# The middle stage of a long convolution, run beside a dense matmul stream: 37 wide items where there were 64 narrow ones, and its last stage moved behind them

## The chip, the cores and the metric

The kernel runs on one core of a Trainium2 chip. TensorE (PE in the profile, PEld for its weight loads), VectorE (DVE), ScalarE (ACT), GpSimd (POOL) and SyncE (SP) run side by side. Each takes its own instructions in a fixed order, and a semaphore holds an instruction until its data is there. SP, ACT and POOL also issue the DMAs. The metric is the device time of one execution in microseconds, as the median of the runs, where lower is better.

## The reference, cut to what matters

The input is 2048 tokens of 576 channels. Two kinds of layer alternate, each twice:

```
def A(x):                                # Fourier mixing of the normalized x
    a, b = x @ dft_hid_re.T, x @ dft_hid_im.T
    return dft_seq_re @ a - dft_seq_im @ b
def B(q, k, v, shift_k, ssm_k, ssm_D):   # q is the normalized x
    kv = shift(k, shift_k) * v           # causal convolution over 4 tokens
    y = irfft(rfft(pad(kv)) * rfft(pad(ssm_k)))[:S] + kv * ssm_D   # long convolution, per channel
    return q * y
x = x + A(norm(x)); x = x + B(norm(x), ...); x = x + A(norm(x)); x = x + B(norm(x), ...)
```

The long convolution `y` depends on k, v and weights alone. It is computed once and used in both B layers.

## The kernel before, in words

**The main stream.** The first A layer (`layer`, called with `get_x0`) takes 128 steps. One step multiplies one block of x by one 128x512 block of the sequence matrix `c_mat`: 14 matmuls of 512 columns (12 into the accumulators `s0` to `s3`, 2 into `rm`). Every product is made of rounded parts: a number is split into a high part (ACT, a copy that rounds) and a low part (DVE, the rest), and three matmuls high x high, high x low, low x high stand for one. The block of `c_mat` for a step is loaded by SP two steps ahead into the ring `craw` and split into the ring `cs` (ACT line 94, DVE line 95). After every 16 steps the accumulators are emptied into `u` by the same kind of split; the remainder `rm` goes through the buffer `rt` at `RT_AT` (lines 270, 271, then a split). `hidden` multiplies a finished block by the hidden matrix: pieces of 27 matmuls of 288 columns, each followed by one DVE add (line 292).

**The branch.** `branch` is a generator that puts the convolution between these steps. Its transform of 4096 points is done as 128 x 16 in three stages.
- First transform: row blocks of k*v and of the filter are multiplied by `f1c` and stored to `t` in DRAM, until the main stream's step 45.
- Middle: an item takes four frequencies q, with 16 j and 2 complex parts on the partitions: `(q j c)` = 128 rows. `mid_kernel` transforms the filter over j (3 matmuls; then ACT copies three half tiles of 64 partitions into `kk`), `mid_signal` transforms the signal (3 matmuls; then four DVE operations form the complex product), `mid_round` splits the product, `mid_inverse` transforms back (3 matmuls, one ACT copy into `vo`) and stores to `vd`. The loaded item itself is split two items ahead (`split_feed`, ACT and DVE).
- Inverse (`i2_products`): one row j of `vd` is split and multiplied by `i2c[j]` (6 matmuls of 288 columns per half of the channels), copied and stored to `yb`.

Before, an item holds one half of the channels, `HD` = 288 columns: 2 halves x 32 groups of four q = 64 items. The inverse takes half rows, 32 of them. Ten half rows of the first half stand between the items of the second half; the other 22 come behind the items. An item's inverse is issued two items after its product (`MID_LAG`).

**What sets the order.** The branch yields a cost; the loop over `layer` resumes it at most `GROUPS` = 2 times at each half step, whenever the branch's costs spent so far are behind the planned share (`spent < work * passed / total`). So the branch is spread evenly from step 47 to step 111. A scheduling layer then fixes the order on each engine. All branch matmuls and the pieces of `hidden` write to one ring of three PSUM banks (tag `b`, names `bk`): a bank is free again when ACT or DVE has read it.

The stage uses two slots for `craw`, laid by these lines; the second is the same memory as `rt`:

```
lay(flts, lay(flts, 8, ("craw", NT, 1)), ("vo", HD, 2))
lay(flts, RT_AT, ("craw", NT, 1))
```

From step 48 on, even steps use the slot at 8 and odd steps the slot at `RT_AT`.

Of the kernel before, what the change touches and what calls it, by code (L numbers as in the profile page):

```python
# [15 lines left out]
P = 128  # L16
# [24 lines left out]
PREP = 113  # L41
MID_LAG = 2
LANDS = 3
BORDER = {J - 1: 0.5, 0: 0.75}
I2_FIRST = 38
I2_LATE = 6
I2_COST = 2.0
GROUPS = 2
# [19 lines left out]
def fnet_h3_kernel(ctx: ExitStack, tc: tile.TileContext, x, c_mat, w_re, w_im, k_pad, v, shift_k,  # L68
# [10 lines left out]
    def bank():  # L79
        return psp.tile([P, NT], F32, tag="b", bufs=3, name="bk")  # L80
# [121 lines left out]

    t_d = [dr.tile([P, J, 2, 2, HD], F32, name=f"t{h}") for h in range(2)]
    v_d = [dr.tile([P, J, 2, HD], F32, name=f"vd{h}") for h in range(2)]
    yb_d = [dr.tile([P, D], F32, name=f"yb{j}") for j in range(J)]
# [149 lines left out]
    def branch():  # L355
# [133 lines left out]
        m1 = region_b(FR, "mid")  # L489
        kk_at = 1976 + 2 * HD + LANDS * D  # L490
        at = lay(m1, 0, ("df", 2 * D, 3), ("mc", 4 * P, 1))
        fresh("land", "fc")
        fresh("craw")
        spare = at
        at = lay(m1, at, ("yf", D, 2))
        lay(m1, at, ("fc", 4 * P, 2))
# [3 lines left out]
        assert at == kk_at  # L500
        assert lay(flts, at, ("kk", D, 2)) <= RT_AT
        mc = quads(ring["mc"]())
        load_fr(mc, midc)
        lo, hi = slice(0, 64), slice(64, 128)

        def mid_half(df, o):
            ps = bank()
            mm(ps[:, :HD], mc[:, 0, :], df[0][:, o:o + HD], True, False)
            mm(ps[:, :HD], mc[:, 0, :], df[1][:, o:o + HD], False, False)
            mm(ps[:, :HD], mc[:, 1, :], df[0][:, o:o + HD], False, True)  # L510
            return ps

        last_act = []

        def act(*args, **kw):
            if last_act:
                with tc.issue_after(last_act[-1]):
                    last_act.append(nc.scalar.activation(*args, **kw).ins)  # L518
            else:
                last_act.append(nc.scalar.activation(*args, **kw).ins)  # L520
# [4 lines left out]

        def mid_kernel(df):
            pk, kk = mid_half(df, HD), two(ring["kk"]())
            act(kk[lo, 0, :], pk[lo, :HD], AF.Copy)
            act(kk[hi, 0, :], pk[lo, :HD], AF.Copy)
            act(kk[hi, 1, :], pk[hi, :HD], AF.Copy)  # L530
            return kk

        def mid_signal(df, kk):
            px = mid_half(df, 0)
            p1, p2 = kk[:, 0, :], kk[:, 1, :]
            nc.vector.tensor_tensor(p1, px[:, :HD], p1, OP.mult)
            nc.vector.scalar_tensor_tensor(p2[lo], px[hi, :HD], -1.0, p2[hi], op0=OP.mult, op1=OP.mult)  # L537
            nc.vector.tensor_tensor(p2[hi], px[lo, :HD], p2[hi], OP.mult)  # L538
            nc.vector.tensor_tensor(p1, p1, p2, OP.add)  # L539
            return p1  # L540

        def mid_round(p1):
            yf = two(ring["yf"]())
            act_split(yf[:, 0, :], yf[:, 1, :], p1)
            return yf

        def mid_inverse(hf, qg, yf):
            pv = bank()
            mm(pv[:, :HD], mc[:, 2, :], yf[:, 0, :], True, False)
            mm(pv[:, :HD], mc[:, 2, :], yf[:, 1, :], False, False)  # L550
            mm(pv[:, :HD], mc[:, 3, :], yf[:, 0, :], False, True)
            vo = ring["vo"]()
            act(vo, pv[:, :HD], AF.Copy)
            nc.scalar.dma_start(v_d[hf][4 * qg:4 * qg + 4].rearrange("q j c d -> (q j c) d"), vo)

        def i2_products(hf, j, fc, vf):
            yo = ring["vo"]()
            ps = bank()
            for c in range(2):
                cs = slice(c * HD, (c + 1) * HD)  # L560
# [6 lines left out]
        mids = [(0, hf, qg) for hf in range(2) for qg in range(32)]  # L567
        late = [(1, 0, j) for j in range(J)]
        feeds = []
        for g, f in enumerate(mids):  # L570
            feeds.append(f)
            if g >= I2_FIRST and (g - I2_FIRST) % 2 == 0 and len(late) > I2_LATE:
                feeds.append(late.pop(0))
        feeds += late + [(1, 1, j) for j in range(J)]
        last_mid = feeds.index(mids[-1])
        rows = [f[2] for f in feeds if f[0]]
        landed, halves, fcs, yfs = {}, {}, {}, []

        def load_feed(i):
            if i < len(feeds):  # L580
                kind, hf, q = feeds[i]
                landed[i] = ring["land"]()
                load_after(landed[i], v_d[hf][:, q].rearrange("p c d -> p (c d)") if kind else
                           t_d[hf][4 * q:4 * q + 4].rearrange("q j c s d -> (q j c) (s d)"))

        def load_fc(k):
            if k < len(rows):
                fcs[k] = quads(ring["fc"]())
                load_fr(fcs[k], i2c[rows[k]])

        def split_feed(i):
            if i < len(feeds):
                halves[i] = parts("df")
                act_split(*halves[i], landed.pop(i))

        for i in range(LANDS):
            load_feed(i)
        yield 0
        for i in range(2):
            split_feed(i)  # L600
            load_feed(i + LANDS)
            load_fc(i)
        used, ahead, product = 0, 2, None
        for i, (kind, hf, q) in enumerate(feeds):
            df = halves.pop(i)
            if kind:
                i2_products(hf, q, fcs.pop(used), df)
                load_fc(used + ahead)
                used += 1
            else:  # L610
                if len(yfs) == MID_LAG:
                    mid_inverse(*yfs.pop(0))
                    yield 0.4
                kk = mid_kernel(df)
                if product is not None:
                    yfs.append((*product[:2], mid_round(product[2])))
                yield 1.6
                product = hf, q, mid_signal(df, kk)
            split_feed(i + 2)
            load_feed(i + ahead + LANDS)  # L620
            if i == last_mid:
                yield 0.4
                mid_inverse(*yfs.pop(0))
                yfs.append((*product[:2], mid_round(product[2])))
                while yfs:
                    yield 0.4
                    mid_inverse(*yfs.pop(0))
                for name, t, at, words in (("fc", m1, spare, 4 * P), ("land", flts, kk_at, D)):
                    old = ring[name]
                    held = [old.tiles[(old.n + m) % len(old.tiles)] for m in range(len(old.tiles))]  # L630
                    fresh(name)
                    lay(t, at, (name, words, 2))
                    ring[name].tiles.extend(held)
                for m in range(2):
                    load_fc(used + ahead + m)
                    load_feed(i + ahead + LANDS + 1 + m)
                ahead = 4
            yield I2_COST if kind else 1.1

# [122 lines left out]
    total = (I2_END + 1 - MID_FROM) * STEP + 3 * 2 * TB * PIECE  # L762
    work = 64 * 3.1 + 32 * I2_COST
    for n, whole in layer(get_x0, lambda j: x[:, j, :], done0, pending):
# [30 lines left out]
        if m == 0:  # L795
            lay(flts, SC_AT + CRAW * NT + 2 * D, ("xa", D, 2), ("yb", D, 2))
            fresh("craw")
            lay(flts, SC_AT + CRAW * NT + 6 * D, ("craw", NT, 1))
# [333 lines left out]
```

## Time and profile before

| | |
|---|---|
| time, median of 3 runs | 1195.03 us (1193.86 to 1195.24) |
| time of the profiled execution | 1196.82 us, of which the span is 1195.0 us |
| PE busy | 1176.4 us, 6320 matmuls |
| DVE busy | 839.1 us |
| ACT busy | 637.3 us |
| middle and inverse stage | 203 to 612 us of the span; the last item's product is formed at 544 us |

The page gives one execution. A line of its group table reads: code line, engine, operation, output <- inputs, shape, count, then busy time and mean duration of one in ns, then the idle time of the engine just before these instructions and what ended it. Matmuls overlap, so the mean duration of one is longer than the step from one to the next.

### The profile page before, as it was taken

The page shows a single profiled execution, that of the slowest core. Times are in us where ns is not written, and L with a number is a line of the kernel's source. Part 1 is how long each engine was busy: PE and PEld are TensorE (multiplying, and loading weights), DVE is VectorE, ACT ScalarE, POOL GpSimd, SP SyncE. Part 2 cuts the span into 40 slices and gives each one's busy share as a digit, 9 for nine tenths or more (in the row PEclk, how much of TensorE's full clock was granted, in tenths as well). Part 3 has the DMA queues.
Part 4 walks back from the last instruction along what each step waited for, and adds up shares of the span by engine and source line. Part 5 has one row for each costly group of instructions (what it writes and reads, how often), then busy time and mean ns, then how long its engine had stood idle before and what let it go on. Part 6 is the DMA issues. An engine that isn't in the chain of part 4 may idle for free.

```text
span 1195.0 us, 18305 instructions
## 1 busy us (share of the span) xinstructions
PE 1176.4 (98%) x6320; PEld 1026.8 (86%) x6320; DVE 839.1 (70%) x1495; ACT 637.3 (53%) x1266; POOL 74.2 (6%) x116
## 2 busy tenths in 40 slices
PE   7999999999999999999999999999999999999997
PEld 6888888987888988888988898788888888889997
DVE  8899794588877678775447665774775776874764
ACT  7965665478766567665435656544444435540210
POOL 2200000000000000001101111000000000001111
PEclk9999999999999999999999999999999999999999
DMA  9889898546666657658947686872592587696621
GB/s 362 277 274 309 259 302 251 180 137 192 196 212 195 196 177 222 185 161 268 300 161 246 224 233 228 275 265 72 160 330 83 159 320 268 202 343 192 214 97 41
DMA packets 150719, 261.97 MB, mean 219 GB/s; under 512 B 16353, under 2 KB 53473, under 8 KB 150626
## 3 DMA queue, kind: packets, MB, share of 16 engines
q1 hardware_dynamic: 107282, 205.58, 53.9%
q10 hardware_dynamic: 36432, 42.63, 10.3%
q0 software_dynamic: 6912, 12.59, 3.9%
q8 instruction: 50, 0.82, 0.3%
q14 instruction: 43, 0.35, 0.1%
HBM read 194.09 MB, written 66.65 MB: 218 GB/s over the span
## 4 chain that ended last, share of the span: by engine, by line
PE 69%; DVE 5%; ACT 3%; DMA 2%; issue 2%; POOL 0%; ACTq 0%; SPq 0%; DVEq 0%; POOLq 0%
PE s L77 38%; PE bk L77 29%; PE rm L77 3%; DVE mid L524 1%; ACT flts L518 1%; DMA flts<-in_c_mat 1%; DVE mats L95 1%; DVE flts L538 1%; ACT mats L94 1%; DMA mid<-in_i2c 0%; DVE flts L537 0%; ACT mid L518 0%; DVE u L95 0%; DMA ph<-in_c_mat 0%; DMA gate<-xa 0%
## 5 line engine op out<-in xcount | busy, mean ns | idle before, releaser
L77 PE MATMUL s<-mats 128*128 128x512 f32 x2088 | 528.6, 392 | 2.0 <-ACT ph L867 1.5
L77 PEld LDWEIGHTS s<-mats 128*128 128x128 f32 x2088 | 380.7, 188 | 72.8 <-ACT ph L867 2.4
L95 DVE TENSOR_TENSOR mats<-flts,mats 128x512 fp32r<-128x512 f32 x201 | 137.3, 688 | 57.5 <-ACT mats L94 50.7
L94 ACT ACTIVATE mats<-flts 128x512 fp32r<-128x512 f32 x201 | 125.8, 627 | 95.2 <-PE bk L77 31.0
L518 ACT ACTIVATE flts<-bk 64x288 f32<-64x288 f32 (+1 forms) x288 | 116.0, 407 | 109.9 <-PE bk L77 93.1
L524 DVE TENSOR_TENSOR mid<-flts,mid 128x576 fp32r<-128x576 f32 (+1 forms) x160 | 102.0, 638 | 47.5 <-ACT mid L518 41.4
L77 PE MATMUL bk<-mid 128*128 128x288 f32 x768 | 128.6, 298 | 2.3 <-ACT flts L518 1.0
L77 PEld LDWEIGHTS bk<-mid 128*128 128x128 f32 x768 | 114.9, 188 | 18.0 <-ACT flts L518 5.8
L77 PE MATMUL bk<-w,u 128*128 128x288 f32 x864 | 120.2, 295 | 0.5 <-DVE flts L292 0.5
L77 PEld LDWEIGHTS bk<-w,u 128*128 128x128 f32 x864 | 117.4, 188 | 3.5 <-DVE flts L292 1.2
L77 PE MATMUL rm<-mats 128*128 128x512 f32 x304 | 94.7, 390 | 0.0
L518 ACT ACTIVATE mid<-flts 128x576 fp32r<-128x576 f32 (+1 forms) x159 | 87.0, 583 | 6.3 <-DVE flts L539 2.2
L454 ACT ACTIVATE flts<-bk 128x288 f32<-128x288 f32 x128 | 50.7, 410 | 47.1 <-PE bk L77 45.2
L77 PE MATMUL bk<-f1r 128*128 128x288 f32 x384 | 64.4, 300 | 6.5 <-ACT f1r L94 6.3
L77 PEld LDWEIGHTS bk<-f1r 128*128 128x128 f32 x384 | 59.4, 191 | 13.0 <-ACT f1r L94 6.6
L77 PE MATMUL bk<-mats 128*128 128x288 f32 (+1 forms) x376 | 67.8, 317 | 0.0
L77 PEld LDWEIGHTS rm<-mats 128*128 128x128 f32 x304 | 56.9, 188 | 12.1 <-ACT flts L518 0.2
L292 DVE TENSOR_TENSOR flts<-flts,bk 128x288 f32<-128x288 f32 x48 | 21.8, 453 | 63.6 <-PE bk L77 63.3
L77 PE MATMUL s<-t,mats 128*128 128x512 f32 x264 | 65.2, 389 | 0.0
L186 POOL TENSOR_TENSOR flts<-flts 128x1 f32<-128x1 f32 x35 | 29.6, 846 | 525.5 <-DVE flts L185 525.5
L77 PE MATMUL bk<-mats,t 128*128 128x288 f32 (+1 forms) x368 | 59.3, 303 | 0.0
L77 PEld LDWEIGHTS s<-t,mats 128*128 128x128 f32 x264 | 49.5, 188 | 10.7 <-DVE mats L200 0.4
(148 smaller groups left out, 1439.3 us busy)
## 6 DMA issues: line engine op xcount, KB each, us to landing
flts<-in_c_mat SPq DMA_DIRECT2D x148, 256.0 KB, 3.9
ph<-in_c_mat SPq DMA_DIRECT2D x54, 512.0 KB, 4.2
t<-flts ACTq DMA_DIRECT2D x64, 288.0 KB, 4.5
flts<-t SPq DMA_DIRECT2D x64, 288.0 KB, 3.2
flts<-in_c_mat SPq DMA_DIRECT2D x30, 512.0 KB, 4.8
vd<-flts ACTq DMA_DIRECT2D x64, 144.0 KB, 3.0
flts<-vd SPq DMA_DIRECT2D x32, 288.0 KB, 3.5
mid<-in_i2c POOLq DMA_DIRECT2D x32, 256.0 KB, 4.9
```

The costliest lines, as they stand in the source:

```text
L77: nc.tensor.matmul(ps, lhsT, rhs, start=first, stop=last, skip_group_check=more)
L94: a = nc.scalar.activation(h, src, AF.Copy).ins
L95: return a, nc.vector.tensor_tensor(l, src, h.bitcast(F32), OP.subtract).ins
L186: pows.append(nc.gpsimd.tensor_tensor(rs, ve, mhalf, OP.pow).ins)
L292: added[:] = [nc.vector.tensor_tensor(rows[hf], rows[hf], ps[:, :HD], OP.add).ins]
L454: stored[:] = [nc.scalar.activation(so[:, c, :], ps[:, :HD], AF.Copy).ins]
L518: last_act.append(nc.scalar.activation(*args, **kw).ins)
L524: nc.vector.tensor_tensor(l, src, h.bitcast(F32), OP.subtract)
L538: nc.vector.tensor_tensor(p2[hi], px[lo, :HD], p2[hi], OP.mult)
```

## The change

The middle stage takes 504 columns at a time: 32 items (one per group of four q) of the first 504 channels, and then 5 items that gather the last 72 channels of 7 groups each (the fifth: of 4 groups, 288 columns). The DRAM tensors `t` and `vd` hold whole rows, so that a store of the gathered items has pieces of 72 values (288 bytes) where one of 504 columns has pieces of 2016 bytes. Wide items are loaded in one buffer (`land`) or, every other one, in two pieces of 504 (`apart`), which are split one by one. An item's inverse is issued one item after its product, where it was two. `vo` has one slot, and `df` two. The inverse takes whole rows of 1152 values in two products of 288 columns, all behind the last item, with two pauses (`MID_PAUSE`) between the last item, the loads and the first row.

Core of the diff:

```diff
-MID_LAG = 2
-LANDS = 3
+MW = 504
+MID_COST = (2.1, 1.7, 1.1)
+MID_PAUSE = 4.0
-I2_COST = 2.0
+I2_COST = 2.3
...
-                nc.scalar.dma_start(t_d[hf][:, j, :, src, :], so)
+                nc.scalar.dma_start(t_d[:, j, :, src, cs], so)
...
-        at = lay(m1, 0, ("df", 2 * D, 3), ("mc", 4 * P, 1))
+        at = lay(m1, 0, ("df", 4 * MW, 2), ("mc", 4 * P, 1), ("yf", 2 * MW, 1))
+        apart = [m1[:, at:at + MW].bitcast(F32), flts[:, 8 + NT:8 + NT + MW]]
-        lay(flts, lay(flts, 8, ("craw", NT, 1)), ("vo", HD, 2))
         lay(flts, RT_AT, ("craw", NT, 1))
-        at = lay(flts, SC_AT + CRAW * NT, ("res", HD, 3), ("vo", HD, 2), ("land", D, LANDS))
+        at = lay(flts, 8, ("craw", NT, 1)) + MW
+        assert lay(flts, at, ("land", 2 * MW, 1), ("kk", MW, 4), ("vo", MW, 1)) <= RT_AT - 3 * HD
...
+        mids = [(q, 1) for q in range(groups)] + [(q, min(per, groups - q)) for q in range(0, groups, per)]
...
+        for n in range(len(mids)):
+            df, w = halves.pop(n), width(n)
+            kk = mid_kernel(df, w)
+            if n:
+                yf = mid_round(product)
+            yield MID_COST[0]
+            product = mid_signal(df, w, *kk)
+            split_mid(n + 2)
+            load_mid(n + 4)
+            yield MID_COST[1]
+            if n:
+                mid_inverse(n - 1, yf)
+                yield MID_COST[2]
+        yf = mid_round(product)
+        yield MID_COST[0]
+        mid_inverse(n, yf)
...
+        yield MID_PAUSE
+        for j in range(3):
+            load_row(j)
+        yield MID_PAUSE
+        for j in range(2):
+            split_row(j)
+            load_row(j + 3)
+        for j in range(J):
+            vf, fc = halves.pop(j), fcs.pop(j)
+            i2_products(0, j, fc, vf)
+            yield I2_COST
+            i2_products(1, j, fc, vf)
+            load_fc(j + 3)
+            split_row(j + 2)
+            load_row(j + 5)
+            yield I2_COST
...
-    work = 64 * 3.1 + 32 * I2_COST
+    work = 37 * sum(MID_COST) + 2 * MID_PAUSE + 32 * I2_COST
```

The two `craw` slots are now laid in the other order: from step 48 on, even steps use the slot that is also `rt`.

The order of TensorE changes within the stage only. The first place is the way from an item's filter transform to the inverse of the item before it. On TensorE before, `bk_3555` and `bk_3564` are filter and signal of item 29, `bk_3583` the inverse of item 27, `bk_3589` and `bk_3608` filter and signal of item 30, and `bk_3619` is the inverse of item 28:

```order
L77 MATMUL bk_3555<-mid_2080 128x288 x3
L77 MATMUL bk_3564<-mid_2080 128x288 x3
L77 MATMUL s2_68<-mats_70 128x512 x3
L77 MATMUL s3_69<-mats_70 128x512 x3
L77 MATMUL rm_3296<-mats_70 128x512 x2
L77 MATMUL bk_3583<-mid_2080 128x288 x3
L77 MATMUL bk_3589<-mid_2080 128x288 x3
L77 MATMUL s0_66<-mats_70 128x512 x3
L77 MATMUL s1_67<-mats_70 128x512 x3
L77 MATMUL bk_3608<-mid_2080 128x288 x3
L77 MATMUL bk_3619<-mid_2080 128x288 x3
```

On TensorE now, `bk_3207` and `bk_3216` are filter and signal of item 17, `bk_3238` is the inverse of item 16, and `bk_3244` the filter of item 18:

```order
L76 MATMUL bk_3207<-mid_2078 128x504 x3
L76 MATMUL bk_3216<-mid_2078 128x504 x3
L76 MATMUL s2_68<-mats_70 128x512 x3
L76 MATMUL s3_69<-mats_70 128x512 x3
L76 MATMUL rm_3102<-mats_70 128x512 x2
L76 MATMUL bk_3238<-mid_2078 128x504
L76 MATMUL bk_3244<-mid_2078 128x504 x3
L76 MATMUL bk_3238<-mid_2078 128x504 x2
```

Between the filter of item n+1 and the inverse of item n there stood 26 matmuls in the first piece, and stand 11 in the second.

The second place is SP's queue where the inverse's rows are loaded. On SP before, a load of a half row (`vd0`) stands among loads of items (`t1`), far behind the stores it needs:

```order
L168 DMA flts_72<-in_c_mat 128x512
L168 DMA flts_72<-t1_78 128x576 x2
L168 DMA flts_72<-in_c_mat 128x512
L697 DMA xa6_103<-flts_72 128x288
L284 DMA flts_72<-in_x 128x288
L168 DMA flts_72<-vd0_79 128x576
L168 DMA flts_72<-in_c_mat 128x512
```

On SP now, the first three whole rows follow the last item's loads, with loads of `c_mat` before and behind them:

```order
L167 DMA flts_72<-in_c_mat 128x512
L167 DMA flts_72<-t_77 128x4x72 x2
L167 DMA flts_72<-in_c_mat 128x512 x9
L167 DMA flts_72<-vd_78 128x1152 x3
L167 DMA flts_72<-in_c_mat 128x512 x2
L167 DMA flts_72<-vd_78 128x1152 x3
```

The first row's load waits for the store of the last gathered item. On TensorE three whole steps, 42 matmuls of 512 columns, stand between that item's inverse and the first row's product.

More of the change, by code (lines that the diff above doesn't have):

```diff
@@ new lines, in branch, with width, load_mid @@
+        per = MW // RW
+        groups = P // 4
+        mids = [(q, 1) for q in range(groups)] + [(q, min(per, groups - q)) for q in range(0, groups, per)]
+        def width(n):
+            first, count = mids[n]
+            return MW if n < groups else count * RW
+        def load_mid(n):
+            if n < len(mids):
+                first, count = mids[n]
+                w = width(n)
+                landed[n] = [r[:, :w] for r in apart] if n % 2 else [ring["land"]()[:, :2 * w]]
+                ends = landed[n] if n % 2 else [two(landed[n][0])[:, i] for i in range(2)]
+                src = t_d[4 * first:4 * (first + count)]
+                if n < groups:
+                    src = src.rearrange("q j c s d -> (q j c) s d")[:, :, :MW]
+                    if n % 2:
+                        for i in range(2):
+                            load_after(ends[i], src[:, i])
+                    else:
+                        load_after(two(landed[n][0]), src)
+                else:
+                    src = src.rearrange("(g q) j c s d -> (q j c) s g d", q=4)
+                    for i in range(2):
+                        load_after(ends[i].rearrange("p (g d) -> p g d", g=count), src[:, i, :, MW:])
@@ new lines, in split_mid, with mid_half @@
+        def split_mid(n):
+            if n < len(mids):
+                df, at = ring["df"](), 0
+                halves[n] = df[:, :2 * width(n)], df[:, 2 * MW:2 * MW + 2 * width(n)]
+                for src in landed.pop(n):
+                    cs = slice(at, at + src.shape[1])
+                    act_split(halves[n][0][:, cs], halves[n][1][:, cs], src)
+                    at = cs.stop
+        def mid_half(df, o, w):
+            ps = bank()
+            mm(ps[:, :w], mc[:, 0, :], df[0][:, o:o + w], True, False)
+            mm(ps[:, :w], mc[:, 0, :], df[1][:, o:o + w], False, False)
+            mm(ps[:, :w], mc[:, 1, :], df[0][:, o:o + w], False, True)
+            return ps[:, :w]
@@ L542, in mid_round, with mid_inverse @@
         def mid_round(p1):
[L543 to L547 removed]
+            w = p1.shape[1]
+            yf = ring["yf"]()
+            yf = yf[:, :w], yf[:, w:2 * w]
+            act_split(*yf, p1)
+            return yf
+        def mid_inverse(n, yf):
+            w = width(n)
             pv = bank()
[L549 to L554, printed above, removed]
+            mm(pv[:, :w], mc[:, 2, :], yf[0], True, False)
+            mm(pv[:, :w], mc[:, 2, :], yf[1], False, False)
+            mm(pv[:, :w], mc[:, 3, :], yf[0], False, True)
+            vo = ring["vo"]()[:, :w]
+            act(vo, pv[:, :w], AF.Copy)
+            first, count = mids[n]
+            dst = v_d[4 * first:4 * (first + count)]
+            if n < groups:
+                nc.scalar.dma_start(dst.rearrange("q j c d -> (q j c) d")[:, :MW], vo)
+            else:
+                nc.scalar.dma_start(dst.rearrange("(g q) j c d -> (q j c) g d", q=4)[:, :, MW:],
+                                    vo.rearrange("p (g d) -> p g d", g=count))
@@ new lines, in branch @@
+        landed, halves, fcs = {}, {}, {}
+        for n in range(2):
+            load_mid(n)
+        yield 0
+        for n in range(2):
+            split_mid(n)
+            load_mid(n + 2)
+        for n in range(len(mids)):
[11 more added lines that the diff above has]
+                yield MID_COST[2]
@@ L591, in split_feed @@
[L591 to L638, printed above, removed]
```

93 lines of the change are left out of this document (38 added, 55 removed).

## The prediction

> **What bounds the kernel now.** I read the page's busy shares first, then the chain that ended last:
>
> ```profile
> span 1195.0 us, 18305 instructions
> PE 1176.4 (98%) x6320; PEld 1026.8 (86%) x6320; DVE 839.1 (70%) x1495; ACT 637.3 (53%) x1266; POOL 74.2 (6%) x116
> ...
> PE 69%; DVE 5%; ACT 3%; DMA 2%; issue 2%; POOL 0%; ACTq 0%; SPq 0%; DVEq 0%; POOLq 0%
> ```
>
> TensorE is the bound: it computes nearly all the time, and the chain lies on it. So the change can move the time in two ways only: by what its matmuls cost, and by the pauses between them. A busy share doesn't show either, since matmuls overlap. For that I take three stretches from the busy time by stretch: the stage that changes, one in which TensorE runs only matmuls of 512 columns, and one with only 288 columns. Columns: the stretch, its length, then busy time and (count) of PE, PEld, DVE, ACT, POOL; granted clock; DMA.
>
> ```profile
> 203.00:612.00 409.00, 406.12 (x2339) 359.67 (x2338) 282.72 (x535) 253.70 (x542) 15.88 (x30) 1.00 0.66 201
> 900.00:1000.00 100.00, 100.00 (x442) 82.79 (x442) 69.45 (x94) 45.57 (x74) 0.00 (x0) 1.00 0.58 191
> 1080.00:1150.00 70.00, 70.00 (x530) 70.00 (x529) 46.69 (x98) 11.56 (x18) 10.16 (x10) 1.00 0.58 183
> ```
>
> The undisturbed step of a matmul is 100.00/442 = 226.2 ns at 512 columns and 70.00/530 = 132.1 ns at 288. The groups of PE in the stage give its matmuls by form:
>
> ```profile
> L77 PE MATMUL s<-mats 128*128 128x512 f32 x798 | 207.3, 392 | 0.1
> L77 PE MATMUL bk<-mid 128*128 128x288 f32 x768 | 128.6, 298 | 2.3 <-ACT flts L518 1.0 <-DVE flts L538 0.3
> L77 PE MATMUL bk<-w,u 128*128 128x288 f32 x639 | 89.1, 295 | 0.5 <-DVE flts L292 0.5
> L77 PE MATMUL rm<-mats 128*128 128x512 f32 x134 | 41.7, 390 | 0.0
> ```
>
> 932 of 512 columns and 1407 of 288 make 932 x 0.2262 + 1407 x 0.1321 = 396.7 us. The stage takes 409.0, so 12.3 us are lost in it. What the weight loads waited for in the same window says to what:
>
> ```profile
> PEld bk L77 <- ACT flts L518: 6.2, 15, 0.8
> PEld bk L77 <- DVE flts L538: 2.2, 6, 0.6
> ```
>
> These are waits for a PSUM bank: a `bk` matmul can't start until ACT's copies (518) or DVE's last read of the signal (538) have emptied the bank of three places earlier. One of them in the timeline:
>
> ```profile
> 270.40 1.24 ACT L518 ACTIVATE flts<-bk 64x288 f32<-64x288 f32 x3
> ...
> 270.56 1.06 PE L77 MATMUL bk<-mid 128*128 128x288 f32 x6 [0.35 <-ACT flts L518]
> ...
> 271.45 0.39 PE L77 MATMUL s<-mats 128*128 128x512 f32 x1
> ```
>
> ACT was late with the copy before these three; PE stood 0.35 us. The six matmuls then took 0.89 us to the next one, not 6 x 0.132 = 0.79: a pause costs another 0.1.
>
> **Matmuls saved.** 64 items of 9 matmuls go (576 x 132.1 ns = 76.1 us). 36 items of 9 at 504 columns and one at 288 come. Between the two steps above a column costs (226.2 - 132.1)/224 = 0.42 ns, so 504 columns are 222.8 ns: 324 x 0.2228 + 9 x 0.1321 = 73.4 us. Saved: 2.7 us. The inverse's 192 matmuls and the main stream stay. This is on the path: PE has nothing beside it.
>
> The Trainium skill, "TensorE: Matmul & The Clock Gate", section "Back-to-back issue gap", gives N/2.4 + 2.5 ns for a warm matmul, 122.5 ns at 288 columns and 212.5 at 504; by it the saving would be 0.6 us and the time 1195.4. The row of 288 columns says 132.1, not 122.5, so I go by the rows.
>
> **ACT, DVE and DMA work saved.** It costs nothing and gains nothing by itself, because PE covers it. What counts is when a bank or a product is ready, and for that I need durations at the new widths. From the groups by shape:
>
> ```profile
> L518 ACT ACTIVATE flts<-bk 64x288 f32<-64x288 f32 x192 | 77.6, 404 | 45.6 <-PE bk L77 29.9 <-DVE flts L538 5.8 <-ACT flts L518 3.2
> L518 ACT ACTIVATE mid<-flts 128x576 fp32r<-128x576 f32 x95 | 64.2, 676 | 2.8 <-DMA flts<-vd 2.1 <-DMA flts<-t 0.7
> L518 ACT ACTIVATE mid<-flts 128x288 fp32r<-128x288 f32 x64 | 28.5, 445 | 3.5 <-DVE flts L539 2.2
> L270 ACT ACTIVATE flts<-rm 64x512 f32<-64x512 f32 x4 | 2.4, 593 | 0.1
> L524 DVE TENSOR_TENSOR mid<-flts,mid 128x576 fp32r<-128x576 f32 x96 | 72.7, 758 | 24.4 <-ACT mid L518 19.5 <-DMA yb<-flts 1.4 <-DMA flts<-in_x 0.7
> L524 DVE TENSOR_TENSOR mid<-flts,mid 128x288 fp32r<-128x288 f32 x64 | 29.3, 458 | 23.2 <-ACT mid L518 21.9
> L536 DVE TENSOR_TENSOR flts<-bk,flts 128x288 f32<-128x288 f32 x64 | 29.1, 455 | 22.6 <-PE bk L77 12.7 <-ACT flts L518 9.7
> ```
>
> ACT: a copy out of a bank 0.59 us at 504 columns (593 ns at 512), a rounding copy 0.80 ns a column more: 0.62 at 504, 1.02 at 1008, 1.14 at 1152. DVE: 1.04 ns a column: 0.68 at 504, 1.21 at 1008, 1.36 at 1152.
>
> **Bank waits that go.** A bank holding the filter is free 0.17 us (298 - 132, the tail of a matmul) and three copies after its last matmul: 0.17 + 3 x 0.404 = 1.4 us before, 0.17 + 3 x 0.59 = 1.9 now. The signal's three DVE reads make 1.5 and 2.2. In the order of PE before, the next use of such a bank stands under 2.7 us of matmuls away in 31 places; now under 3.1 us in 10. With 8.4 us of these waits (6.2 + 2.2), I keep a third, 2.7, and count 5.7 as gone. Bounds: 2 (ACT and DVE can be late for other reasons) to 8.4.
>
> **New waits.** (1) The shorter lag. The inverse of item n needs the rounded product, which ACT makes behind the three filter copies of item n+1: 0.17 + 3 x 0.59 + 0.62 = 2.56 us after that filter's last matmul. The order leaves 3 x 0.2228 + 8 x 0.2262 = 2.48 us in three items, one matmul less, 2.25, in four, 2.9 in one, 3.6 or more in all others (before: at least 4.1, need 1.8). 3 x 0.1 + 4 x 0.3 + 7 x 0.1 of restart = 2.2 us. Bounds: 0, if ACT's copies start early, to 5, if DVE's half of the rounding comes late too.
>
> (2) The `rt` slot. A block of `c_mat` for it can be loaded only when the remainder of a finished accumulation has left `rt`. Before, that hit the fourth step after it (51, 83, 115), now the third (50, 82, 114). Before, at the quiet boundary (step 111 ends with `rm`) and the busy one (step 47):
>
> ```profile
> 616.06 0.61 PE L77 MATMUL rm<-mats 128*128 128x512 f32 x2
> ...
> 619.60 0.81 SPq L168 DMA_DIRECT2D flts<-in_c_mat  x2
> 622.31 0.63 ACT L94 ACTIVATE mats<-flts 128x512 fp32r<-128x512 f32 x1 [3.46 <-DMA flts<-in_c_mat]
> 622.86 2.88 PE L77 MATMUL s<-mats 128*128 128x512 f32 x12
> ...
> 250.82 0.62 PE L77 MATMUL rm<-mats 128*128 128x512 f32 x2
> 257.49 0.81 SPq L168 DMA_DIRECT2D flts<-in_c_mat  x2
> ```
>
> The first block was split at 622.94. Step 114, which now uses it, began at 622.86: 0.1 late. At the busy boundary the load went 6.7 us after `rm`; with the same 2.7 us to landing and 0.63 for the split that is 10.0 us, where the new order has 9.4 us of matmuls. 0.7 each at steps 50 and 82: 1.5 us in all, bounds 0 and 4 (a load queued behind others on SP).
>
> (3) From the last item to the first row. Three steps of 14 matmuls cover it: 42 x 0.2262 = 9.5 us. The path: a copy, the store to `vd`, the load of a whole row on SP, the split. Issues to landing:
>
> ```profile
> vd<-flts ACTq DMA_DIRECT2D x64, 144.0 KB, 3.0
> flts<-vd SPq DMA_DIRECT2D x32, 288.0 KB, 3.5
> mats<-wd SPq DMA_DIRECT2D x9, 576.0 KB, 6.1
> flts<-y SPq DMA_DIRECT2D x4, 64.0 KB, 4.6
> ```
>
> Low: 0.17 + 0.41 + 3.0 + 3.5 + 1.14 = 8.2 us, no wait. High: a store of 288-byte pieces takes 4.6, as the loads of 256-byte pieces (`y`) do, a row of 576 KB takes 6.1: 12.4, and the low parts on DVE 1.36 more, 13.8: 4.3 late. `c_mat` loads queue behind the row loads on SP, but these steps have theirs two ahead. I take 2.5, nearer the high end, since the store has the small pieces and `vo` a single slot.
>
> The Trainium skill, "DMA: Bandwidth & Descriptors", section "Specifications", names 512 bytes as the least transfer for line rate and a read-modify-write below it, which speaks against the gathered items; the `y` row (64 KB in 4.6 us) agrees that small pieces are no faster.
>
> (4) The first split of the stage is wider: 1.02 + 1.21 us against 0.68 + 0.76. 0 to 0.8, I take 0.5.
>
> **Sum.** -2.7 - 5.7 + 2.2 + 1.5 + 2.5 + 0.5 = -1.7 us. The span goes from 1195.0 to 1193.3, the profiled time from 1196.82 to 1195.1. The median shown (1195.03) lies 1.8 under the profiled run, so the prediction is 1195.03 - 1.7 = 1193.3. A difference under 0.2% (2.4 us) is about what a measurement of this kernel can't tell from none; this sum is inside it.
>
> **Rivals.** *The pauses go* (faster). The banks are emptied in fewer, longer pieces, and the new waits stay hidden apart from 1.5 us: -2.7 - 5.7 + 1.5 = -6.9, 1188.1 us. For it: only 7 of 37 items have a distance below the need. Against: a pause seldom vanishes without another wait behind it.
>
> *The lag decides* (slower). If the chain from the filter of item n+1 to the rounded product of n takes 3.56 us and not 2.56, because another split stands on ACT or DVE ahead of it, the eight nearest inverses wait 4 x 1.3 + 3 x 1.1 + 0.6 + 8 x 0.1 = 9.9 us in place of 2.2: 1201.0 us. It decides against the change from about 0.5 us of delay on. For it: DVE has little room,
>
> ```profile
> 203.00:530.00 327.00, 324.37 (x1840) 285.30 (x1839) 246.76 (x477) 217.23 (x468) 5.29 (x10) 1.00 0.63 189
> ```
>
> 246.76/327 = 75% while the items run, and the change packs them into less time. Against: per item DVE takes 4 x 0.68 + 0.68 + 1.21 = 4.6 us at 504 columns against 3.0 at 288, 170 us against 194, so its share stays near this.
>
> *The width saves nothing*: if 504 columns cost as much per column as 288 do (132.1/288 = 0.459 ns), the 2.7 us are not there: 1196.0. Against: the step at 512 is 0.442.
>
> **Chances.** The sum as it stands 0.42, its own range 1190.6 to 1196.0, of which 0.13 is faster by over 0.2%, 0.26 within, 0.03 slower. Pauses go 0.26, all faster. The lag decides 0.26, all slower. Width saves nothing 0.06, nearly all within. Together: faster 0.39, same 0.31, slower 0.30. The range runs from a little under the fast rival to a little over the slow one, 1187.5 to 1201.5.
>
> **What would show it.** Right: 324 matmuls of 504 columns at steps near 223 ns, weight-load waits for line 518's and 538's successors under half of 8.4 us, short waits for the rounded product in seven items, pauses at steps 50 and 82, and one of some 2.5 us before the first row's product; a stage that ends about 2 us sooner. Wrong: a pause in every item before the inverse (the lag), a first-row wait of 5 us or more, or waits for `c_mat` splits over 2 us each.

## The result, and the profile after

| | before | changed |
|---|---|---|
| time, median of 7 runs each | 1195.21 us (1193.47 to 1196.43) | 1199.85 us (1197.67 to 1204.45) |
| ratio, 95% interval | | 1.0045 (1.0028 to 1.0061) |

The changed kernel is slower by 0.45%, some 4.6 us, where 1193.3 us was forecast, with "faster" as the likeliest outcome (0.39). The page of the changed kernel:

```profile
span 1195.9 us, 17258 instructions
PE 1177.1 (98%) x6077; PEld 1010.8 (85%) x6077; DVE 815.5 (68%) x1335; ACT 614.5 (51%) x1106; POOL 66.1 (6%) x100
...
PE 87%; DVE 4%; DMA 4%; ACT 3%; issue 1%; SPq 0%; POOLq 0%; DVEq 0%; POOL 0%; ACTq 0%
```

This span is only 0.9 us over the 1195.0 of before. A profile is one execution: the first of before was 1.8 us above its median, this one is the fastest of its seven. So I took a second profile of each, unaltered (`before_again`, span 1192.2 us; `again`, 1196.4 us). They differ by 4.2 us, nearly what the medians do (4.6), and the comparison below uses them.

By the page nothing is wrong: TensorE (PE) computes 98% of the time as before, and every engine does less. The stage shows it. The busy time by stretch, of `before_again` and then of `again` (columns as in the prediction):

```profile
203.00:612.00 409.00, 406.80 (x2344) 360.57 (x2343) 284.05 (x536) 255.04 (x544) 15.91 (x30) 1.00 0.66 202
```

```profile
203.00:612.00 409.00, 405.20 (x2076) 341.09 (x2074) 259.93 (x375) 230.56 (x382) 8.45 (x16) 1.00 0.62 191
```

DVE and ACT have 24 us less to do in the same 409 us, and PE stands more. What its weight loads waited for in that stretch, in the first profile after (total, times, longest):

```profile
PEld bk L76 <- ACT mid L505: 5.5, 10, 0.9
PEld bk L76 <- ACT flts L505: 3.9, 10, 0.5
PEld bk L76 <- DVE mid L509: 3.2, 7, 1.1
PEld bk L76 <- DVE flts L566: 2.6, 5, 1.2
```

The two `flts` rows are the bank waits (6.2 and 2.2 before). The two `mid` rows are waits for rounded numbers, 8.7 us together, where the first profile of before has 1.0.

For the size of the pauses I take each matmul's start from the trace, subtract the start before it and the undisturbed step (132.1, 222.8 and 226.2 ns for 288, 504 and 512 columns), and sum what is left by the matmul that came late. Second profiles, us, 203 to 612 us unless said:

| late matmul | before | changed | difference | predicted |
|---|---|---|---|---|
| filter and signal of an item | 4.7 | 4.5 | -0.3 | -5.7 |
| inverse of an item | 1.1 | 3.8 | +2.8 | +2.2 |
| main stream, with 612 to 640 | 0.8 | 2.1 | +1.3 | +1.5 |
| row products | 0.6 | 1.8 | +1.3 | +2.5 |
| pieces of `hidden` | 0.8 | 0.7 | -0.1 | +0.5 |
| under 0.04 each | 3.5 | 5.4 | +1.8 | 0 |
| outside 203 to 640 | 8.0 | 8.7 | +0.7 | 0 |

Together +7.5, less 2.7 of undisturbed steps: +4.8 between first and last matmul (1177.9 and 1182.7 us).

### The profile page after: what moved, and what is told of

It reads as the page before. It is cut to its first block, busy times and chain, and to the rows that moved or that the text cites. A ratio compares the mean times of both kernels' runs of the same rounds, so it can differ in the third digit from the quotient of the medians.

```text
span 1195.9 us, 17258 instructions
## 1 busy us (share of the span) xinstructions
PE 1177.1 (98%) x6077; PEld 1010.8 (85%) x6077; DVE 815.5 (68%) x1335; ACT 614.5 (51%) x1106; POOL 66.1 (6%) x100
## 4 chain that ended last, share of the span: by engine, by line
PE 87%; DVE 4%; DMA 4%; ACT 3%; issue 1%; SPq 0%; POOLq 0%; DVEq 0%; POOL 0%; ACTq 0%
PE s L76 49%; PE bk L76 33%; PE rm L76 5%; DMA flts<-in_c_mat 1%; DVE mid L509 1%; ACT flts L505 1%; ACT mid L505 1%; DMA vd<-flts 1%; DVE mats L94 1%; DVE flts L182 0%; DMA wd<-w 0%; DVE flts L565 0%; DVE flts L566 0%; DMA flts<-in_ssm_k 0%; DMA flts<-vd 0%
## 5 line engine op out<-in xcount | busy, mean ns | idle before, releaser
L76 PEld LDWEIGHTS s<-mats 128*128 128x128 f32 x2088 | 386.1, 188 | 80.8 <-ACT ph L896 1.7
L505 ACT ACTIVATE flts<-bk 64x504 f32<-64x504 f32 (+3 forms) x180 | 98.3, 551 | 103.0 <-PE bk L76 92.2
L76 PE MATMUL bk<-mid 128*128 128x504 f32 (+1 forms) x525 | 123.4, 359 | 3.7 <-ACT mid L505 1.3
L509 DVE TENSOR_TENSOR mid<-flts,mid 128x1008 fp32r<-128x1008 f32 (+3 forms) x90 | 81.5, 906 | 52.9 <-ACT mid L505 51.6
L76 PEld LDWEIGHTS bk<-mid 128*128 128x128 f32 x525 | 86.9, 188 | 26.3 <-ACT mid L505 5.5
L505 ACT ACTIVATE mid<-flts 128x1008 fp32r<-128x1008 f32 (+3 forms) x90 | 71.4, 798 | 21.8 <-PE bk L76 15.9
L76 PEld LDWEIGHTS bk<-mats 128*128 128x128 f32 x376 | 55.6, 188 | 3.4
```

The costliest lines, as they stand in the source:

```text
L76: nc.tensor.matmul(ps, lhsT, rhs, start=first, stop=last, skip_group_check=more)
L509: nc.vector.tensor_tensor(l, src, h.bitcast(F32), OP.subtract)
```

## The experiments

All kernels compute the whole result. Medians; "before" ran beside each call at 1194.6 to 1194.9 us.

**again and before_again**: no edit.

> The changed kernel itself, unaltered, for a second profile beside the first: the first was taken in an execution of 1197.67 us, the fastest of seven whose median is 1199.85. Every theory expects a median of 1198.5 to 1201 us, 4 to 5.5 us over the kernel before. What differs is where the second profile, if it is one of the slower executions, carries its extra 1 to 4 us: by the lag theory in longer waits ahead of the inverse of items 4, 16, 18, 20, 23, 25 and 28 (in the first profile 3.8 us with their restarts); by the c_mat theory in the first steps of an accumulation (50, 82, 114: in the first profile together about 1.6 us); by the transfer theory ahead of the first row's product (1.7 us in the first profile) and outside the stage.

> The kernel before, unaltered, for a second profile: the first has a pause of 2.4 us near 740 us, outside the stage, which the changed kernel's does not show. If that pause belongs to one execution only, the second profile lacks it and the difference of the traces grows by some 1 to 2 us to what the medians show (4.5 us); if it is in both, the traces keep showing less than the medians, and the rest is in executions without a profile.

Measured: `again` 1199.6 us (1198.17 to 1199.91), ratio 1.0042 (1.0030 to 1.0054). `before_again` 1193.97 us; the pause near 740 us belonged to the first execution only (2.65 us lost in 700 to 760 us there, 0.23 here). The second profile of the changed kernel was again one of its quick executions, so where the slower ones carry their extra was not seen.

**slot**: the order of the two `craw` slots as before.

```diff
-        lay(flts, RT_AT, ("craw", NT, 1))
         at = lay(flts, 8, ("craw", NT, 1)) + MW
+        lay(flts, RT_AT, ("craw", NT, 1))
```

> Two lines swapped: the slot at 8 is laid ahead of the one at RT_AT, so that even steps use the slot at 8 again, as before. If the rt slot is a cost, the late s0 of steps 50, 80 and 82 (in the first profile some 1.6 us with their restarts) goes back to step 83 with a smaller one, and the time falls by 1 to 2 us, to 1198 to 1199. By the lag theory alone it stays within 0.7 us of the changed kernel.

**before_swap**: the kernel before with the other slot order.

```diff
-        lay(flts, lay(flts, 8, ("craw", NT, 1)), ("vo", HD, 2))
         lay(flts, RT_AT, ("craw", NT, 1))
+        lay(flts, lay(flts, 8, ("craw", NT, 1)), ("vo", HD, 2))
```

> The kernel before with one thing of the change alone: the slot at RT_AT is laid first, so that even steps use it from step 48 on. If the slot order by itself is what made the change slower (it took 4.8 us away there when undone), the kernel before becomes 3 to 5 us slower, 1198 to 1200. If the order costs only the late s0 of steps 50, 82 and 114, as the prediction had it, it becomes 1 to 2 us slower, 1196 to 1197. If it hurts only together with the wide items (ACT held at a late split of c_mat with three longer copies and a longer rounding behind it), it stays within 0.7 us.

Measured: `slot` 1194.78 us (1193.42 to 1195.5), ratio to before 1.0000 (0.9991 to 1.0008): 4.8 us less than `again`, all of the loss. `before_swap` 1198.26 us, 3.6 over before by the medians, ratio 1.0024 (1.0013 to 1.0034), which is 2.9. So two swapped lines account for the result, and for more than the late first steps that the prediction counted. At step 50 in the timeline of `again`:

```profile
264.14 0.81 SPq L167 DMA_DIRECT2D flts<-in_c_mat  x2
...
267.17 0.63 ACT L93 ACTIVATE mats<-flts 128x512 fp32r<-128x512 f32 x1
...
267.85 0.97 PE L76 MATMUL s<-mats 128*128 128x512 f32 x3 [0.19 <-ACT mats L93]
```

and in `slot`:

```profile
212.01 0.43 SPq L167 DMA_DIRECT2D flts<-in_c_mat  x1
...
261.98 0.62 ACT L93 ACTIVATE mats<-flts 128x512 fp32r<-128x512 f32 x1
```

In `slot` the block lies there 50 us ahead and is split 5 us before PE needs it; in `again` the load goes when `rt` is empty, and the split ends as the step begins. Call lead the time from the end of a block's split on ACT to the step that uses it: step 50 loses 4.9 us of lead, and the next three steps have 0.3, 3.3 and 2.3 us less than in `slot`. Steps 82 and 114 lose 5.0 and 4.8 us in the same way. The starts of the steps show where the time goes: `again` falls behind `slot` by 1.4 us at steps 50 to 53, 0.7 at step 67, 0.9 at steps 83 to 86 and 0.4 at 114 and 115, in each case three to seven steps behind a finished accumulation. At step 60 it gains 0.9 back. The waits of ACT for a block, from 203 to 640 us, tell how often a split then stands at the head of ACT's queue without its data. In `before_again`, `before_swap`, `again` and `slot`, in this order:

```profile
ACT mats L94 <- DMA flts<-in_c_mat: 8.2, 7, 3.5
```

```profile
ACT mats L94 <- DMA flts<-in_c_mat: 19.1, 13, 4.3
```

```profile
ACT mats L93 <- DMA flts<-in_c_mat: 17.4, 13, 3.5
```

```profile
ACT mats L93 <- DMA flts<-in_c_mat: 12.7, 9, 3.4
```

ACT takes its queue in order, so the filter's copies and the roundings wait behind such a split. The largest case, in the timeline of `before_swap`, behind the boundary at step 80:

```profile
463.62 0.33 SPq L168 DMA_DIRECT2D flts<-in_c_mat  x1
...
468.55 0.63 ACT L94 ACTIVATE mats<-flts 128x512 fp32r<-128x512 f32 x1 [4.29 <-DMA flts<-in_c_mat]
469.20 0.41 ACT L518 ACTIVATE flts<-bk 128x288 f32<-128x288 f32 x1
...
469.67 0.67 PE L77 MATMUL bk<-mid 128*128 128x288 f32 x3 [1.99 <-ACT flts L518]
```

A block that PE itself doesn't need yet holds ACT for 4.29 us, the copy behind it frees its bank late, and PE stands 1.99 us for the bank. In the kernel before, the bank waits grow with the swap from 8.1 to 11.2 us (weight loads, lines 518 and 538, 203 to 612 us).

In the changed kernel they don't. The weight loads of `slot`, 203 to 612 us:

```profile
PEld bk L76 <- ACT mid L505: 4.8, 9, 0.7
PEld bk L76 <- ACT flts L505: 3.7, 10, 0.5
PEld bk L76 <- DVE flts L566: 3.0, 5, 1.2
PEld bk L76 <- DVE mid L509: 2.2, 5, 1.1
```

The bank waits are 6.7 us here and 6.8 in `again`: `again` waits for banks at 276 and 281 us, behind a split that held ACT for 3.05 us, and `slot` waits as long at 310 us, where `again` does not. What the order changes is the waits for rounded numbers, 7.0 us here and 8.8 in `again`, and those for splits of `c_mat`, none here and 1.0 in `again`. Start to start, `slot` saves 2.3 us between the first and the last matmul: 1.1 in the main stream and 1.1 at inverses. So the copy that frees its bank late is shown for the kernel before; in the changed kernel the traces show late blocks and late roundings. Undoing the order shortened the span by 2.8 us under the profile and the median by 4.8; the other 2 us are in executions without a profile, and what makes them stays open.

**lag and lag_slot**: the costs spread so that no inverse is near, without and with `slot`.

```diff
-MID_COST = (2.1, 1.7, 1.1)
+MID_COST = (2.1, 2.8, 0.0)
```

> One line: the costs that an item yields are (2.1, 2.8, 0.0), not (2.1, 1.7, 1.1). Their sum is the same, but the inverse of item n now stands at least 2.9 us of matmuls behind the filter of item n+1 (2.26 to 2.49 us for seven items in the changed kernel), where 2.56 us are needed. If the short lag is what costs, the waits ahead of the inverses (3.8 us in the first profile) go and the time falls by 3 to 4.5 us, to 1195.5 to 1197. If the bank ring or the c_mat slot decide, it falls by less than 1 us, since the filter of the next item now follows the inverse at once and one gap from a signal to the next filter shrinks to 0.7 us. If 504 columns at 228 ns and transfers are the loss, nothing moves (within 1 us).

> Both edits together, the costs (2.1, 2.8, 0.0) and the slot order of before. If both waits are real and independent the gains add up, 4 to 6.5 us, to 1193.5 to 1196, level with the kernel before or a little faster. If one wait only passes to the other (a later inverse meets a later split of c_mat), the sum is no more than the larger of the two, 3 to 4 us.

Measured: `lag` 1196.35 us, 3.3 less than `again`; `lag_slot` 1196.07, level with `lag` and 1.3 over `slot`. The seven short waits are gone, but inverses of items 4, 8 and 12 now wait 1.2 to 1.5 us each, the last two for a bank. From the timeline of `lag`:

```profile
286.54 0.68 DVE L565 SCALAR_TENSOR_TENSOR flts<-bk,flts 64x504 f32<-64x504 f32 x1
287.38 0.63 ACT L93 ACTIVATE mats<-flts 128x512 fp32r<-128x512 f32 x1 [2.16 <-DMA flts<-in_c_mat]
...
288.56 0.68 DVE L509 TENSOR_TENSOR mid<-mid 128x504 fp32r<-128x504 f32 x1 [1.34 <-ACT mid L505]
...
289.28 0.68 DVE L566 TENSOR_TENSOR flts<-bk,flts 64x504 f32<-64x504 f32 x1
...
290.10 1.16 PE L76 MATMUL bk<-mid 128*128 128x504 f32 x4 [1.34 <-DVE flts L566]
```

Here ACT waits for a late block, a split on DVE (509) waits for ACT, and it stands ahead of the third read of the signal (566), which frees the bank. One late transfer passes through two queues to PE. So `lag` doesn't measure the lag alone.

**slot_round**: `slot`, with the rounding ahead of the next filter.

```diff
-            kk = mid_kernel(df, w)
             if n:
                 yf = mid_round(product)
+            kk = mid_kernel(df, w)
```

> The changed kernel with the slot order of before and with the rounding of item n-1's product issued ahead of the filter of item n, so that ACT makes it before the three copies of that filter. If the lag is a real cost, the waits ahead of the inverses (2.7 us with the slot order of before, 3.3 with what follows them) mostly go: 1 to 3 us faster than that kernel's 1194.8, 1192 to 1193.8. If ACT's and DVE's queues only pass the wait on, the filter's copies come later by the rounding and the bank waits grow by as much: 1194.3 to 1196.

Measured: 1193.77 us, ratio 0.9995 (0.9985 to 1.0004): 1.0 under `slot`. Pauses at inverses fell only from 2.7 to 2.1 us, so this edit takes away a part of what the lag costs; with the other edits (`slot_all`, below) they fall to 1.3. Another part is only passed on: the weight loads' waits for rounded numbers fell from 7.0 to 4.0 us, and those for banks rose from 6.7 to 7.1.

**slot_pause**: `slot` with `MID_PAUSE = 6.0`.

> The changed kernel with the slot order of before and MID_PAUSE 6 in place of 4: between the last item's inverse and the first row stand 12.7 us of matmuls, not 9.5. If the store, the row's load and its split take 11 to 12 us, as the first profile has it (pauses of 1.5 to 1.9 us ahead of the first row), these go: 1 to 2 us faster than 1194.8, and up to 0.9 more since the new spread leaves four short lags, not seven. If ACT or DVE is late there for other work, it stays within 0.5 us.

Measured: 1196.77 us, 2.0 slower than `slot`. The wait for the first row went (1.8 us lost in 500 to 530 us, now 0.2), but the items, packed into less time, met other waits: 400 to 480 us lost 6.2 us, 4.0 in `slot`. The wait is real, and cheaper than what its cover costs.

**slot_narrow**: `slot` with 64 items of 288 columns.

```diff
-MW = 504
-MID_COST = (2.1, 1.7, 1.1)
+MW = 288
+MID_COST = (1.21, 0.98, 0.64)
...
-    work = 37 * sum(MID_COST) + 2 * MID_PAUSE + 32 * I2_COST
+    work = 64 * sum(MID_COST) + 2 * MID_PAUSE + 32 * I2_COST
```

> The changed kernel with the slot order of before and MW 288: 64 items of 288 columns in the changed kernel's structure (shorter lag, whole rows behind the last item), with the item's costs scaled to the same total. It isolates the width. If the prediction's first two terms hold (2.7 us of matmuls and 5.7 us of bank waits saved by the width), it is about 8 us slower than the same at 504 columns (1194.8): 1202 to 1204. If the width brings what the traces seem to show (steps of 504 columns at 228 ns, so 1 us of matmuls, and bank waits only passed on), it is 0 to 2.5 us slower: 1194.8 to 1197.3. If it is faster than 1194, the wide items cost more in waits than they save.

**before_lag1**: the kernel before with the shorter lag alone.

```diff
-MID_LAG = 2
+MID_LAG = 1
```

> The kernel before with MID_LAG 1 in place of 2, nothing else. By the prediction's way of counting (need 0.17 + 3 x 0.404 + 0.445 = 1.83 us after the filter's last matmul, distances of 1.53 to 2.2 us in the tight places) only some four inverses are 0.1 to 0.3 us late: 1 to 2 us slower, 1196 to 1197. If other splits stand on ACT and DVE ahead of the rounding, as the narrow kernel's trace has it (14.2 us of pauses ahead of the inverses, 1.1 us in the kernel before), it is 6 to 12 us slower: 1201 to 1207.

Measured: `slot_narrow` 1204.64 us (1204.15 to 1206.15), 9.9 slower than `slot`; `before_lag1` 1203.16 us (1201.16 to 1203.41), ratio 1.0068 (1.0054 to 1.0082), 8.5 slower than before. The weight loads' waits, 203 to 612 us, of `slot_narrow`, `before_lag1` and `before_again`:

```profile
PEld bk L76 <- ACT mid L505: 14.9, 26, 1.3
PEld bk L76 <- DVE mid L509: 6.4, 23, 0.4
PEld bk L76 <- ACT flts L505: 1.5, 5, 0.5
...
PEld bk L76 <- DVE flts L566: 0.4, 2, 0.2
```

```profile
PEld bk L77 <- ACT mid L518: 10.9, 21, 1.1
PEld bk L77 <- DVE mid L524: 3.5, 14, 0.4
PEld bk L77 <- ACT flts L518: 1.7, 3, 0.9
...
PEld bk L77 <- DVE flts L538: 0.4, 2, 0.2
```

```profile
PEld bk L77 <- ACT flts L518: 5.9, 14, 0.7
PEld bk L77 <- DVE flts L538: 2.2, 6, 0.6
...
PEld bk L77 <- ACT mid L518: 0.4, 1, 0.4
```

At 288 columns nearly all is waits for the rounded product: pauses ahead of inverses sum to 14.2 us in `slot_narrow` and 9.4 in `before_lag1`. Beside these kernels the width brings 10 us, but mostly by paying for the lag that came with it: fewer inverses, and more matmul time between them. The bank waits of before (8.1 us together) are down to 1.9 us in `slot_narrow` and 2.1 in `before_lag1`, though their items are as narrow as before. A likely reason, which no run tests, is that PE already stands at the inverse and the bank is free by then. Waits of one kind give way to another.

**slot_reads, slot_first, slot_all, all_rt**: `slot` with splits behind the signal's reads; with the first row in halves; with both and the rounding; and the last with the changed slot order.

```diff
             act(h, src, AF.Copy)
-            nc.vector.tensor_tensor(l, src, h.bitcast(F32), OP.subtract)
+            with behind(*last_read[-1:]):
+                nc.vector.tensor_tensor(l, src, h.bitcast(F32), OP.subtract)
...
-            nc.vector.tensor_tensor(p2[hi], px[lo], p2[hi], OP.mult)
+            last_read.append(nc.vector.tensor_tensor(p2[hi], px[lo], p2[hi], OP.mult).ins)
...
-                act_split(*halves[j], landed.pop(j))
+                src = landed.pop(j)
+                if j:
+                    act_split(*halves[j], src)
+                else:
+                    for hf in range(2):
+                        act_split(*[v.rearrange("p (c h d) -> p c h d", c=2, h=2)[:, :, hf] for v in (*halves[j], src)])
```

> The changed kernel with the slot order of before, and the DVE half of a split is issued behind the last of the three reads of the signal that stands ahead of it in the program. Of 37 items, 35 have a split of 0.68 to 1.2 us between the second and the third read of the signal's bank now; here 17 have. If DVE's order is what holds the banks, the two pauses of 0.8 to 0.9 us ahead of the filters of items 2 and 13 go, and the time falls by 1 to 2.5 us, to 1192.3 to 1193.8. If the splits that come later then make the next products late, nothing is gained: 1194.3 to 1196.

> The changed kernel with the slot order of before, and the first row is split in two halves of the channels, so that the first product needs 576 values of each part and not 1152. Ahead of the first row TensorE stands 0.48 us for ACT's half and 0.93 us for DVE's. If the transition's wait is a real cost, 0.9 to 1.3 us of it go: 1193.5 to 1194. If it is not on the path, no change within 0.5 us.

> Slot order of before, the rounding ahead of the next filter, the split behind the signal's reads, and the first row in halves, all together. No split but one then stands between a signal's reads on DVE. If these waits are separate, the gains add: 1.0 (rounding first, measured) and 1 to 2.5 and 1: 1190.5 to 1192, 3 to 4 us under the kernel before. If each only passes its wait to another queue, it stays where the rounding alone is: 1193 to 1194.5.

> The same four edits as the fastest kernel so far (rounding ahead of the filter, splits behind the signal's reads, first row in halves), but with the changed kernel's slot order, in which even steps use the slot that is also rt. If the slot order is a cost of its own, it is 3 to 5 us slower than 1191.2: 1194.2 to 1196.2. If it acts only where the items leave ACT and DVE no room, it is less than 2 us slower: 1191.2 to 1193.

Measured: `slot_reads` 1192.92 us, ratio 0.9984 (0.9976 to 0.9993), 1.9 under `slot`; its bank waits are 4.4 us, where `slot` has 6.7. `slot_first` 1194.31, 0.5 under `slot`, not to be told from it. `slot_all` 1191.2 us (1189.42 to 1192.93), ratio 0.9968 (0.9956 to 0.9980): 3.4 us under before, the fastest here; the gains add (3.6 under `slot`, the three alone 1.0, 1.9 and 0.5). In its stage the weight loads waited

```profile
PEld bk L76 <- ACT flts L505: 3.0, 6, 1.0
PEld bk L76 <- DVE flts L291: 2.2, 7, 0.4
PEld bk L76 <- DVE mid L510: 1.6, 5, 0.6
PEld bk L76 <- ACT mid L505: 1.4, 3, 0.7
```

`all_rt` took 1192.15 us: the same slot order that cost 4.8 us in the changed kernel costs 1.0 here by the medians, 1.8 by the two ratios to before (0.9983, with an interval from 0.9973 to 0.9993, against 0.9968), whose intervals overlap. And ACT's wait for blocks is longer than anywhere, in a profile of the slowest of its executions (1195.79 us):

```profile
ACT mats L93 <- DMA flts<-in_c_mat: 25.0, 13, 5.0
```

Even so PE lost 13.6 us from 203 to 640 us, where it lost 18.2 in `again`. So ACT's waiting is not itself the cost. It costs where a bank or a rounded product that PE needs soon is queued behind it, on ACT or one queue further on DVE.

## Why the prediction was wrong

Measured and forecast lie 6.5 us apart. Two terms of the sum failed by much; one was measured by an edit undone, the other by the table, so their misses overlap and do not add up to the 6.5.

**The `rt` slot, new wait (2): 1.5 predicted, 4.8 found** by undoing it, over its upper bound of 4 (2.3 between the first and the last matmul of two profiles). Alone in the kernel before it cost 3.6. Its place was right: steps 50 and 114 begin 0.05 us after their splits on ACT end, step 82 0.6 us after. The step that failed is "0.7 each at steps 50 and 82": it counted the first step that uses the slot and nothing behind it, neither the lead missing in the next splits nor the copies and roundings queued behind a late split on ACT.

**Bank waits that go: -5.7 predicted, -0.3 found,** the largest miss in the table. Two things failed. The 8.4 us are waits of the weight load, which begin before PE is out of work (2.41 against 1.99 us at 469.67 us in `before_swap`); start to start the late filters and signals of before cost 4.7 us, so 5.7 could not go. And I counted distances by nominal times, with no other work between a bank's reads. In `slot`, 35 of 37 items have a split on DVE between the second and third read of the signal; with 17 (`slot_reads`) the time fell 1.9 us.

**Matmuls saved: -2.7 predicted, -0.9 found.** Interpolation between two undisturbed stretches gave 222.8 ns for 504 columns. By form there are 324 of them in the stage, as foreseen. Six of 504 and six of 512 in the timeline of the changed kernel, with the row of the groups that gives the length of one:

```profile
L76 PE MATMUL bk<-mid 128*128 128x504 f32 x324 | 91.8, 399 | 2.4 <-DVE flts L566 1.1 <-ACT mid L505 0.7 <-DVE mid L509 0.2
```

```profile
344.74 1.55 PE L76 MATMUL bk<-mid 128*128 128x504 f32 x6
...
346.13 1.55 PE L76 MATMUL s<-mats 128*128 128x512 f32 x6
...
347.71 0.62 ACT L505 ACTIVATE mid<-flts 128x504 fp32r<-128x504 f32 x1 [0.28 <-DVE flts L567]
...
348.39 1.18 PE L76 MATMUL bk<-mid 128*128 128x504 f32 x4 [0.25 <-ACT mid L505]
...
349.02 0.68 DVE L509 TENSOR_TENSOR mid<-flts,mid 128x504 fp32r<-128x504 f32 x1
...
349.76 0.72 PE L76 MATMUL bk<-mid 128*128 128x504 f32 x2 [0.19 <-DVE mid L509]
```

(1.55 - 0.40)/5 = 0.230 us for either; the median in the stage is 229 ns for both. The step that failed is taking 226.2 ns from the undisturbed stretch: in the stage 512 columns took 228 ns (median) before the change too. The 212.5 ns worked out from the Trainium skill, "TensorE: Matmul & The Clock Gate", section "Back-to-back issue gap", which gives its formula for an isolated matmul, is not borne out. 229 ns is near the rival "the width saves nothing" (0.459 x 504 = 231 ns), which was given 0.06.

**The lag, new wait (1): 2.2 predicted, 2.8 found.** Its place was exact: the seven items foreseen (4, 16, 18, 20, 23, 25, 28) wait ahead of their inverses. The last four rows show item 16: the rounding starts at 347.71, PE waits for ACT's part and again, at 349.76, for DVE's. In `slot` no inverse started under 2.91 us after its filter's last matmul did, 2.69 after that one's step, where 2.56 was worked out; DVE's part was only in the upper bound. So the rival "the lag decides" (1201.0 us, 0.26) came near the time for a reason that isn't its own. Its mechanism is real at 288 columns (`before_lag1`, 8.5 us); at 504 it takes about 3.

**From the last item to the first row, (3): 2.5 predicted, 1.3 found,** in the place foreseen. The reason given, stores in small pieces, is not what the trace shows: the five gathered stores landed in 2.6 to 4.3 us, the 32 wide ones in 2.0 to 4.9, and the first row's load took 3.9, not 6.1. The single `vo` slot does count: ACT's copy of the last item waited 1.41 us for the store before it. The first row in the changed kernel:

```profile
505.11 1.16 ACT L505 ACTIVATE mid<-flts 128x1152 fp32r<-128x1152 f32 x1 [2.04 <-DMA flts<-vd]
506.30 2.76 DVE L509 TENSOR_TENSOR mid<-flts,mid 128x1152 fp32r<-128x1152 f32 x2 [2.51 <-ACT mid L505]
506.32 0.40 PE L76 MATMUL bk<-mid 128*128 128x288 f32 x1 [0.53 <-ACT mid L505]
...
507.72 0.92 PE L76 MATMUL bk<-mid 128*128 128x288 f32 x5 [0.77 <-DVE mid L509]
```

**(4), the wider first split,** cost nothing that can be seen (pieces of `hidden` 0.8 before, 0.7 now). That PE is the bound, and that ACT's and DVE's saved work gains nothing by itself, held: 24 us less on each, and a slower kernel.

## What to carry to other kernels

When a change touches which buffer a prefetch uses, count how many steps ahead each load can go, and follow a late one through every in-order queue to what is queued behind it; here the main stream, its first consumer, had 1.1 of the 2.3 us that the traces show. Price waits by the starts of the waited-for matmuls, not by the weight load's waits, and don't let a whole class of waits go by distances that leave out other work on the engine that must free the bank. Where a change packs several edits, run the kernel with each of the small ones undone: here two swapped lines hid that the rest was level with before, and three small edits more made it 3.4 us faster than before.

## What the runs showed of the hardware that was not expected

In this stage, where matmuls of 288, 504 and 512 columns alternate, 504 and 512 columns step alike at 229 ns (median), while 512 alone stepped at 227 ns (median; 226.2 as a mean) in 900 to 1000 us. The 504 columns are not the cause: without them, in the kernel before, the same stage has 228 ns. What is stays open. A profiled execution lay between 2.2 us under its kernel's median (the changed kernel) and 3.6 over it (`all_rt`), and with that moves the price of the same edit (2.8 us under the profile, 4.8 in the medians).
